# One order of issue exchanged for another in an attention and Mish feed-forward kernel

## The chip, the core and the metric

The kernel runs on one core of one Trainium2 chip. The metric is device time in microseconds (us), from one timed execution to the next of the same program; the kernel before was timed three times, and the median counts. One more execution was recorded by the hardware profiler, and all readings of single instructions come from that one.

A core has engines that run side by side, each through its own list of instructions in the order in which they were issued: PE (TensorE, matrix multiplication; its weight loads are listed as PEld), DVE (VectorE), ACT (ScalarE), POOL (GpSimd) and SP (SyncE, which here only starts transfers). An engine waits at the first instruction of its list whose inputs aren't there; nothing behind it can overtake.

## The reference, cut to what matters

Attention over hashed buckets, then a feed-forward layer with the Mish function between two matrices:

```python
B, H, S, D = 4, 8, 768, 64                       # q, k, v: float32; proj: 64 x 6
q_bits = (q @ proj > 0); k_bits = (k @ proj > 0) # 6 bits: one of 64 buckets
mask = q_bucket[:, :, :, None] == k_bucket[:, :, None, :]
scores = where(mask, q @ k.T / sqrt(D), -1e9)
attn = exp(scores - scores.max(-1)); attn /= attn.sum(-1) + 1e-9
x = (attn @ v) as 3072 x 512
h = x @ w_in                                     # 512 x 2048, float64 in memory
g = h * tanh(log1p(exp(h)))                      # Mish
out = g @ w_out                                  # 2048 x 512, float64 in memory
```

## The kernel before, in words

Every matrix operand is held as two float16 parts, a high part ("hi") and the remainder ("lo"), and a product is made of two or three matmuls of these parts. The two weight matrices arrive as 64-bit numbers, and are put together into float32 on the chip first (operations `w_u`, `w_sign`, `w_low`, `w_join`), then scaled by a power of two and split (`square`, `st`, `half`, `w_hi`, `w_lo`). The same scaling and splitting is done for q, k and v (`k_hi`, `k_lo`, and so on). A bucket's bits go through a small matmul (`hp`), and turn into columns of large constants beside q and k (`bits`), so that the mask is part of the score matmul.

The attention is cut into 96 slots. A slot n has two heads and 128 queries against 768 keys. In the order of the data:

- `S`n, on PE: 8 matmuls into the PSUM tile `ps_s`, of which there is only one (line 802). The next `S` has to wait until both `exp` of this one have read it.
- `max`, on DVE: a maximum over 2 x 768 scores (line 809), and from it a scale and a bias (lines 812 and 815). There are two forms of the last part: for both heads in one instruction each, or for one head at a time, with twice the instructions.
- `exp`, twice, on ACT (line 825), each with its row sums. Results go to a ring of three buffers `pb`.
- `sums` and `rv` (lines 838 to 847): one over the sums.
- `hi`, twice: the scaled float16 part, on ACT (line 368), POOL (line 366) or DVE (line 369), to a ring of three buffers `hl`.
- `lo`, twice: the remainder. For the first ten slots PE makes it (`diag`, `lo_pe`, lines 415 and 416) and ACT or DVE copies it out of PSUM. From slot 10 on it is one instruction on DVE (line 387), or two on POOL (lines 393 and 394).
- `ptturn`, twice: a transposing transfer from `hl` to `PT`, started by SP (line 428).
- `V`p, on PE, for each two slots: 36 matmuls (line 882); `x_hi` on ACT and `x_lo` on DVE take the result out.

Eight slots make a unit of 256 tokens, and there are 12 units. A unit then goes through the feed-forward layer in eight groups m of 256 hidden columns: `H`m on PE (24 matmuls, lines 913 to 915), `mish` on ACT (line 931), `g_hi` on ACT, POOL or DVE, `g_lo` on DVE (line 387), and `O`m0 and `O`m1 on PE (6 matmuls each, lines 951 to 953). `exp` and `mish` are in different function tables of ACT; each change between them costs a table load, which the trace shows as an instruction of its own.

The program doesn't issue anything while it describes this. Each operation is entered into a list with the operations it must follow and with its alternatives, one for each engine or form that can do it. The description makes 2,671 operations, numbered in the order of the description. `ORDER` (line 87) is a text that was written by a planner ahead of time: a row of these numbers, each with a letter for its alternative (none for the first, b, c, d). `Plan.ordered` goes through that text and issues, without any other reordering:

```python
for w in ORDER.split():
    n, a = (int(w[:-1]), "abcd".index(w[-1])) if w[-1].isalpha() else (int(w), 0)
    o = self.ops[n]
    assert all(q in done for q in o.preds), o.name
    done.add(o)
    yield o.alts[a][2]
```

So `ORDER` sets the order of each engine's list, the order of SP's transfers, and the engine of every operation that has a choice. For instance, "24c" is the split of q for the first unit on its third alternative, DVE. `S8` is 344 in that row, `S20` is 758, `S92` is 2515, and the first feed-forward matmul `H0` is 470.

Of the kernel before, what the change touches and what calls it, by code (L numbers as in the profile page):

```python
# [92 lines left out]
121 193c 148c 227b 159 194 77 166b 206b 195b 108 147 149 150 197 182 160 257 198 183 207 196 201 78 161 228 199b
202 162 208 184b 203 209b 210 167 173 164 151 180 174 94 200 229 217b 221 213b 186 211b 176b 238 222 214 212c
204 223 218 185b 163 187 224 175c 219b 241c 253 258b 215 165 242 177 239 240 188 254b 216 189 243b 259 420 178
249b 245 230 260 255 246 256 244c 286 220 250 251 287 237 282 270d 271 272c 274c 231 191 275 283b 299 233c 236
232 247 343 276 285 288c 278 284 269 300 252 234 190 289 248 277 297 302 318b 273b 303 305b 301 235b 298 310c
192 314 290 279 304b 280 315b 306b 261 291 292 281 311 316 307 308 309 293c 262 317 294c 268 312b 319 320b 295
331c 263 264 378 344 296 379 332 333 321 334c 359 339b 330 340 335b 380 322 265 360 341 336 345 329 313 346 348c
361 337 347 381 323 362 266 267 324 338 363 325c 326b 364c 374 327 382 342 349 389 383 366b 370 407b 350c 390  # L100
365c 328 384 351 386c 371 367 408b 352 385b 409 353 372b 368 354 369 355 375 447b 376 432 410 356c 377 387 448
391 449c 392 394c 450 433 411 357 419 466 388 418 403 395b 434 393b 358 467 399 412 413 451 396 485b 414 468
415b 421 404 486 457 400 397 487 422 456 405 406 416 401b 511c 373 417 469 398 443 435b 488 470 402 489 495 436
423 437b 494 444 438 439 478 445 446 425 441 440 458c 481 512 426 513 424 479 459 480 461b 482 471 474 442 460
452 464 475 453 427 462 472c 465 428 535 514 473 631 483 476 490 430 429 484 546b 496b 463 515 507 454 491 521
497 504 539 498 492 499 508 505 500 509 510 455 520 522c 547 502 501 540 431 523 531 541 548b 516 524 549 525
517 550 493 477 557 551 558b 552 553b 526 559 518b 530 554 560b 503 532 542 519 561 593 562 536 556 506 533 543
537b 563 564 624 555 545 534 565c 583c 544 567c 575 566 584 576 579 528 538 585b 568 614 586 569 527 587 571b
580b 570 529 581 582 606c 588 589 592 590c 573 597b 591 594 598 595c 607 572 599b 577 596 628 578 629 600 609b
574 608 601 632 633 610 634 651 620 630 602 635 603 652 617 636 611 616 612 621 653 604c 637 746 654 605 647 613  # L110
638b 675 648 655 615b 656 640 625 657c 676 721 679 649 618 659 650 619 683 622c 623 626c 677b 690 658 641 666
667 639 684 660 668 686 627 685 642b 687 720 691 645 674 644 688 692 670 750 693 643 694c 671 696 697 661 662
689 703c 669 663 747 680 664 704 716 678 646 717b 751 665 711 672b 748 706 705 681b 754 698 709 682 712 707 718
719 695b 699 735d 736 758 713 701 722 723 749 752 724 700 673 759 737 760 725 739 726 743 744 728 770 773c 714
708 710 702 774 761 785 755 753 740 738c 775 789 771 776 729 762 766 772 727b 783 730 778c 763 756b 777 791 741
784 790 757 767 786b 731 732 779 792 733 793 745 764b 787 742 788 734 812 794 795c 820 797 804d 815 765 805 780
816b 823b 821 814 798 781b 813 715 838 806 870 768b 817 808 818 807c 824 769 825b 782 822 809 796 839 840 810b
826 834 835 827c 819 829 836 865 799 866 837 800 841 924 878 802 833 874 879b 867 811 828b 831b 871 857 801 842
843 875 868b 844 832 882 853 858 869 830 803 880 859b 854 861 846 886 847 883 887 881 855 872c 903 884 890 905
860 885 873 891 895d 896 892 862 845b 863b 904 848 906 925 897 907 849 899 918 908 876 898 926 927 909c 856 928c  # L120
850 864 937 930 910 917 888b 901b 911 920 921 900 922 851 889 913 931 938 919 939 902 852 914 923 943d 912 940
915b 951 1144 944 932 954 941b 955 945c 969 956 947 957 916 933 970 929b 946c 973 977 949 950 978b 934 948 971b
966 972 1262 974 1055 981 952 1100 958 959 967 975 960c 877 962 979 893c 980 961 982 1000 983b 992b 1001 963
1101 976 894 964 985 1002 986 993 994c 1014 984 1003 1102 995b 1103 996 965 1004 998 1005 987c 1015 935 1104c
988 1021 1016 989 990 1017 1006b 1007 1008b 1033 1010b 1018b 1046 997 991 999 1020 1106b 1019 1025 1051 1034
1026 1009c 1011 1052 1047 1048 1035b 1028b 1012b 1027c 1029 1036 1037 1031 1022 936 1023 1038 1143 1060 1049c
1024 1039 1105b 1056 1107 1145 1013 1061 1050 1064 1053b 968 1062 1080 1065 1030 1108 1057 1041 1079 1032 1040b
1263 1109 1058 1054 1042 1059 1292 1068 942 1081 1071b 1044 1066b 1264 1072 1093 953 1063 1265 1073 1069 1094
1082b 1110 1075 1083 1095 1111 1043 1074b 1325 1084 1113 1070 1266 1067 1045 1085b 1086 1087 1076 1077 1096 1267
1125 1097 1089 1114 1088c 1098 1099 1078 1115 1091 1112 1090 1117c 1140 1118 1116 1128 1150 1141 1119b 1129 1121  # L130
1126b 1268 1092 1146 1120c 1123 1130 1142 1131 1270b 1132c 1154 1166 1151 1147 1155 1148c 1133 1232 1134c 1167
1152 1149 1136 1122 1135c 1269c 1153 1156 1157 1169d 1170 1162 1124 1138b 1178 1163 1171b 1127 1177 1137 1168
1179 1158 1139 1159 1180b 1172b 1192 1175b 1191 1173 1160c 1164b 1224 1181 1182 1194 1183 1225 1161 1193 1199
1195 1184 1196 1185c 1165 1228 1187 1226c 1197 1202c 1211 1200 1201 1174 1186b 1203 1210 1176 1189 1198 1204
1206b 1212b 1188 1205 1213 1214 1237 1233 1190 1229 1227 1215b 1207 1208 1216 1218b 1256 1217b 1230b 1238 1234b
1245 1231 1219 1209 1235 1236 1246 1241 1221 1239 1248b 1242 1258 1247 1285 1249 1223 1257 1240 1259b 1243c 1244
1220 1250 1251 1286 1252 1271 1222 1260 1287 1254b 1261 1288 1277d 1293 1272 1278 1273 1279 1253 1289 1255 1281
1290 1274 1291 1280b 1305 1306 1282 1307 1317 1320 1309 1310 1312 1283b 1308 1321 1311c 1313 1284 1322 1350 1323
1315 1275 1351 1339d 1340 1354 1341b 1294 1358 1318b 1295 1347 1355 1324 1352 1296b 1362 1314 1348 1359b 1316
1349 1298 1353 1356 1366 1343 1360 1370 1342c 1345 1383 1474 1357 1363 1367 1299 1364 1365 1361 1373c 1385 1371  # L140
1368b 1276 1344 1372 1375c 1376 1412 1297b 1326 1300 1377b 1386 1378 1301 1384 1379 1303 1327 1328 1346 1302
# [952 lines left out]
```

## Time and profile before

| | before |
|---|---|
| device time, median of 3 runs (lowest to highest) | 886.45 us (886.02 to 888.27) |
| span of the profiled execution, first to last instruction | 887.0 us |
| busy time of PE, DVE, ACT, POOL in it | 823.2, 679.0, 606.0, 301.4 us |
| mean granted clock of TensorE | 0.987 of full speed |

The profiled execution's own time is its span, 887.0 us; the median of the timed runs is 0.55 us below it, and nothing of the execution lies outside the span that this argument needs. A row of the groups of instructions reads: line of the kernel, engine, operation, output <- inputs, shapes, count | busy us, mean ns of one | idle time of the engine just before them, and what ended most of it. A row of the stretches gives for a stretch of time its length, then the busy us and the count of instructions of each engine (PE, PEld, DVE, ACT, POOL), the granted TensorE clock, the busy share of the transfer engines, and GB/s. A row of a timeline gives start, duration, engine, line, operation and names.

### The profile page before, as it was taken

To read this page: it belongs to the slowest core of one execution; us is meant where nothing else is said; L and a number is where in the kernel's file an instruction comes from. 1 tells how busy PE (TensorE), PEld (TensorE's weight loads), DVE (VectorE), ACT (ScalarE), POOL (GpSimd) and SP (SyncE) were. 2 spreads that over 40 slices of the span, in tenths; PEclk is the share of its full clock that TensorE was granted. 3 is DMA by queue.
4 is the path that set the end of the run, shared out by engine and by line. 5 is a ranking of instruction groups with operands and counts; after the bars stand their busy time and mean duration, and the time that the engine had idled before them with its cause. 6 is when DMAs were issued, how large, how long until landed. Compare 5 with 4: busy or idle time off the path is not lost.

```text
span 887.0 us, 17219 instructions
## 1 busy us (share of the span) xinstructions
PE 823.2 (93%) x6626; PEld 547.1 (62%) x6626; DVE 679.0 (77%) x1323; ACT 606.0 (68%) x963; POOL 301.4 (34%) x279
## 2 busy tenths in 40 slices
PE   3689988889999999999899999999989999999998
PEld 1355555566666767656657666766756766776665
DVE  3688799998778888778888987678888777776421
ACT  6686878887788676768677667756867657666410
POOL 3353442223442515333144413443332523335000
PEclk9799999999999999999999999999999999999999
DMA  8999989689999797567999968669999667566300
GB/s 266 270 230 246 213 220 207 143 193 175 219 154 180 132 210 141 105 119 149 209 208 185 184 108 155 108 124 219 211 184 166 121 130 138 102 106 134 72 24 24
DMA packets 432690, 143.75 MB, mean 162 GB/s; under 512 B 402912, under 2 KB 423392, under 8 KB 432608
## 3 DMA queue, kind: packets, MB, share of 16 engines
q1 hardware_dynamic: 432608, 142.65, 81.5%
q8 instruction: 52, 0.85, 0.4%
q14 instruction: 30, 0.25, 0.1%
HBM read 35.65 MB, written 6.29 MB: 47 GB/s over the span
## 4 chain that ended last, share of the span: by engine, by line
PE 50%; DVE 14%; DMA 8%; ACT 7%; issue 5%; POOL 2%; SPq 1%; ACTq 0%; DVEq 0%; POOLq 0%
PE ps_s L802 9%; PE ps_acc L913 6%; PE ps_acc L914 6%; PE ps_acc L915 6%; PE ps_t L882 6%; PE ps_o L951 6%; PE ps_o L953 5%; PE ps_o L952 5%; DVE svb L809 5%; ACT pb L825 4%; DMA PT<-hl 3%; DMA QT<-tok 3%; DMA KT<-tok 2%; DVE hl L387 2%; DVE svb L812 1%
## 5 line engine op out<-in xcount | busy, mean ns | idle before, releaser
L825 ACT ACTIVATE pb<-ps_s,svb 128x768 f32<-128x768 f32 x192 | 189.1, 987 | 118.9 <-DVE svb L815 104.0
L913 PE MATMUL ps_acc<-X,wi 128*128 128x256 f16 x768 | 211.2, 275 | 2.5 <-ACT ffb L931 2.4
L914 PE MATMUL ps_acc<-X,wi 128*128 128x256 f16 x768 | 211.2, 275 | 0.0
L915 PE MATMUL ps_acc<-X,wi 128*128 128x256 f16 x768 | 211.2, 275 | 0.0
L809 DVE TENSOR_REDUCE svb<-ps_s 128x2 f32<-128x1536 f32 x96 | 168.5, 1755 | 41.8 <-PE ps_s L802 39.8
L802 PE MATMUL ps_s<-KT,QT 128*128 128x512 f16 (+1 forms) x768 | 142.8, 329 | 17.7 <-ACT pb L825 16.2
L953 PE MATMUL ps_o<-wo,ffb 128*128 128x512 f16 x384 | 145.5, 379 | 0.4 <-DVE ffb L387 0.3
L951 PE MATMUL ps_o<-wo,ffb 128*128 128x512 f16 x384 | 145.8, 380 | 0.0
L952 PE MATMUL ps_o<-wo,ffb 128*128 128x512 f16 x384 | 145.5, 379 | 0.0
L387 DVE SCALAR_TENSOR_TENSOR hl<-pb,svb,hl 128x768 f16<-128x768 f32 x125 | 135.6, 1090 | 6.5 <-POOL hl L366 3.5
L366 POOL TENSOR_SCALAR hl<-pb,svb 128x768 f16<-128x768 f32 x63 | 65.2, 1036 | 221.1 <-DVE svb L847 88.7
L802 PEld LDWEIGHTS <-QT 128*128 128x128 f16 x768 | 73.2, 98 | 73.6 <-issue 27.6
L882 PE MATMUL ps_t<-PT,VT 128*64 128x256 f16 x1728 | 103.7, 274 | 1.3 <-DVE hsum L670 0.7
L931 ACT ACTIVATE ffb<-ps_acc,smalls 128x512 f32<-128x512 f32 x96 | 64.1, 684 | 59.1 <-PE ps_acc L915 52.6
L882 PEld LDWEIGHTS <-VT 128*64 128x64 f16 x1728 | 91.1, 110 | 18.5 <-issue 18.4
L387 DVE SCALAR_TENSOR_TENSOR ffb<-ffb,smalls 128x512 f16<-128x512 f32 x96 | 73.9, 774 | 27.1 <-POOL ffb L366 20.3
L368 ACT ACTIVATE hl<-pb,svb 128x768 f16<-128x768 f32 x73 | 67.5, 929 | 29.0 <-DMA PT<-hl 16.4
L914 PEld LDWEIGHTS <-wi 128*128 128x128 f16 x768 | 75.7, 99 | 17.6 <-issue 3.7
L913 PEld LDWEIGHTS <-wi 128*128 128x128 f16 x768 | 75.7, 99 | 13.1 <-issue 1.6
L915 PEld LDWEIGHTS <-wi 128*128 128x128 f16 x768 | 75.8, 99 | 9.4
L394 POOL TENSOR_TENSOR hl<-pb,hl 128x768 f16<-128x768 f32 x47 | 79.8, 1697 | 3.9
L393 POOL TENSOR_SCALAR pb<-pb,svb 128x768 f32<-128x768 f32 x47 | 46.3, 986 | 90.4 <-ACT hl L368 53.1
(177 smaller groups left out, 1086.9 us busy)
## 6 DMA issues: line engine op xcount, KB each, us to landing
out_dram<-ffb SPq DMA_DIRECT2D x24, 256.0 KB, 3.0
stg<-in_k_dram SPq DMA_DIRECT2D x12, 384.0 KB, 4.4
stg<-in_v_dram SPq DMA_DIRECT2D x12, 384.0 KB, 4.1
stg<-in_q_dram SPq DMA_DIRECT2D x9, 512.0 KB, 5.1
wi<-in_moe_w_in_dram SPq DMA_DIRECT2D x7, 512.0 KB, 4.1
wo<-in_moe_w_in_dram SPq DMA_DIRECT2D x6, 512.0 KB, 5.2
stg<-in_moe_w_out_dram SPq DMA_DIRECT2D x6, 512.0 KB, 5.7
PT<-hl SPq DMA_TRANSPOSE x192, 4.0
```

The costliest lines, as they stand in the source:

```text
L387: return [("DVE", 215 + 1.035 * n, port(lambda: nc.vector.scalar_tensor_tensor(out=dst, in0=src, scalar=sc, in1=hi, op0=ALU.mult, op1=ALU. ...
L394: nc.gpsimd.tensor_tensor(out=dst, in0=src, in1=hi, op=ALU.subtract)
L802: nc.tensor.matmul(ps_s[:, hh * S + c0 * P:hh * S + c1 * P], QTb[:, u % 2, sl, qi], KTb[:, j, sl, hh * NCH + c0:hh * NCH + c1].rearrange(" ...
L809: nc.vector.tensor_reduce(out=sv[:, 0], in_=ps_s.rearrange("p (h e) -> p h e", h=2), axis=AX.X, op=ALU.max, negate=True)
L825: EXP[n, hh] = op("exp", [("ACT", 1075, lambda hh=hh, t=t: nc.scalar.activation(pb[:, t], ps_s[:, hh * S:(hh + 1) * S], AF.Exp, bias=sv[:, ...
L882: nc.tensor.matmul(pv[hh * D:(hh + 1) * D, 0:256], vt[:, w, hh * NCH + c], pt[:, hh, a * NCH + c].rearrange("p s t -> p (s t)"), start=(x ...
L913: nc.tensor.matmul(o, wh, X[:, 0, c], start=(c == 0), stop=False)
L914: nc.tensor.matmul(o, wh, X[:, 1, c], start=False, stop=False)
L915: nc.tensor.matmul(o, wl, X[:, 0, c], start=False, stop=(c == NCC - 1))
L951: nc.tensor.matmul(PS[f"o{s}"], gh, wo[:, g, 0, f2], start=first, stop=False)
L952: nc.tensor.matmul(PS[f"o{s}"], gh, wo[:, g, 1, f2], start=False, stop=False)
L953: nc.tensor.matmul(PS[f"o{s}"], gl, wo[:, g, 0, f2], start=False, stop=last)
```

## The change

The text of `ORDER` is replaced as a whole. The description of the operations, their instructions, what each must follow, the tiles and the rings stay as they are, so the instructions of PE and the transfers are the same set. The diff has some 120 lines on each side that look alike; these are the first of both sides and the last:

```diff
 ORDER = """
-3 12 1 6 0 7 8 2 13 14 9 53 10 79 54 17 18 20 21 19 35 15 4 5 24c 63 22 11 25 16 23 56 26 48b 55 99 47b 38b 111c
-60 36b 64 27 65 37c 28 59 66 89b 91 80c 112 92 39 81b 29 82 40 41 30 156 83 31 32 33 113b 42 67 43 44 49 68 45
...
-2628 2631 2629 2630 2632 2633b 2639 2640 2643 2615 2634 2644 2641 2642 2645c 2646 2659 2660 2647 2651 2648 2649
-2652 2650 2653 2662 2661 2655 2654 2664 2663 2656 2657c 2658 2665 2668 2666b 2669b 2667 2670
+12 7 6 156 4 3 13 8 17 14 53 54 15 55 56 60 16 57 20 21 0 1 2 9 5 10 18 19 24 35 26c 27 22 23 28b 36c 63 64
+38c 65 66 48c 99 79 67 111b 37c 39 40 68 25 80c 81c 11 29 30 47c 49 92 31 33 91 58 41 42 32 43 44 59 112b 113
...
+2646 2656 2657c 2652 2653c 2658 2615 2618 2659 2660 2661 2662 2654 2663 2664 2665 2666b 2667 2668 2669b 2670
 """
```

Counted over the two texts, these are the choices that differ most (number of operations in each place, before -> after):

| operation | ACT | DVE | POOL |
|---|---|---|---|
| `hi` (192) | 73 -> 55 | 56 -> 51 | 63 -> 86 |
| `lo` from slot 10 on (172) | - | 125 -> 91 | 47 -> 81 |
| `g_hi` (96) | 35 -> 19 | 29 -> 43 | 32 -> 34 |
| remainders of k, q, v and weights, `k_lo` `q_lo` `v_lo` `w_lo` (48) | - | 43 -> 27 | 5 -> 21 |
| high parts `k_hi` `q_hi` `v_hi` `w_hi` (60) | 23 -> 13 | 24 -> 19 | 13 -> 28 |
| `w_u`, `w_low` (34) | 16 -> 11 | 9 -> 8 | 9 -> 15 |
| `diag` (32) | 15 -> 7 | 7 -> 13 | 10 -> 12 |
| `max`, both heads at once / one at a time | - | 47 / 49 -> 67 / 29 | - |

In ACT's new list a change between `exp` and `mish` occurs 91 times, in the old one 75 times. The relative order on PE changes too: `H`, `O`, `V` and `S` follow one another in another sequence, with the first `H` after `S11` in both. Of the 350 transfers that SP starts, 67 stand in the same place of its list.

More of the change, by code (lines that the diff above doesn't have):

```diff
@@ L93 @@
[L93 to L117, printed above, removed]
@@ new lines @@
+811 814 819 836 837 840 857c 799 800 801 869 865 878 872 802 831b 924 841 842 843 858 879b 859 880 861 881
+895c 896 745 803 830 860 832 844 846b 886 833 890 905 882 903 891 847 863 897c 899 892 906b 848 845 887 873
+849 862 864 898b 893 901 900 902 925 883 904 926 917 918 907 908 927 884b 909c 853 885 910 920 937 938 919 911
+888b 928 921 922 913 930b 931 914 1100 889 850 912c 923 939 940 943c 944 945c 954 955b 947b 957 915 956 894
+973 854 855 856 958b 877 851 946b 969 949b 974 970 971 977 916 948 715 852 932 978 933 959 960b 962 929c 972
@@ new lines @@
+1402 1520 1504 1569 1521 1513 1522 1523 1447 1448 1543c 1494 1484c 1449 1485 1403 1445 1525 1512b 1515b 1544
+1488c 1489 1518 1554 1519 1537 1526 1573 1555 1319 1514 1516 1545b 1547b 1546 1527 1528c 1451 1450 1452 1548
+1557 1556 1558d 1477 1453 1559 1577 1566 1570 1581 1454 1574 1549 1530 1531 1578 1575 1585 1579 1455 1567b
+1571c 1541c 1560b 1562b 1580 1561 1550 1563 1532 1551 1542 1592 1593 1533 1572 1602 1603 1529 1564b 1456 1552
+1586 1582 1583 1604 1594c 1576 1535 1595c 1596 1587b 1584 1600 1601 1589 1590 1591 1565 1700 1615 1614 1605
@@ new lines @@
+2174 2049 2158b 2051 2119 2137 2126 2177 2114 2116 1949 2146b 2149 2076 2150 2148 2127 2050 2170 2171 2159
+2160 2178 2128b 2130b 2161b 2179 2162 2180 2192b 2193 2166 2185 2054 2181 2055 2056 2172 2343 2202 2052 2163
+2131 2194b 2182 2186 2195 2189 2190 2167 2129c 2151 2203 2191 2344 2196b 2205 2093c 2094 2164 2197 2165 2251
+2201 2132 2198b 2199 2300 2133 2204 2152 2206c 2183b 2207 2175 2176 2134 2141 2187 2135 2209b 2217 2218 2219
+2208b 2210 2220 2225 2226 2184 2212b 2200 2215 2222 2223 2227 2301 2234 2224 2142 2136 2211 2255 2188 2235b
@@ new lines @@
+2366 2334 2351 2320 2336 2357 2367 2358 2362 2295 2348c 2368 2352 2323b 2349 2356 2369 2370 2153 2168 2337
+2372 2375b 2379 2363 2359 2341b 2353 2325 2378 2324 2380 2339 2381 2424 2371b 2360 2373 2382 2383 2384 2326
+2392 2376 2374 2394 2361 2395 2385b 2386 2396 2399 2377 2428 2387b 2388 2397 2389b 2402b 2310 2403 2411 2390
+2312 2412b 2391 2400 2429 2425 2441 2437 2413 2430c 2401 2426c 2427 2404b 2406b 2405b 2364c 2408 2414 2415c
+2433 2365 2416 2417c 2407 2327 2418 2434 2419b 2435 2436 2445 2393 2446 2421b 2342 2409 2420 2422 2398 2410
```

180 lines of the change are left out of this document (94 added, 86 removed).

## The prediction

> **What bounds the kernel now.** I read the page first, for the engines' shares of the profiled execution.
>
> ```profile
> span 887.0 us, 17219 instructions
> PE 823.2 (93%) x6626; PEld 547.1 (62%) x6626; DVE 679.0 (77%) x1323; ACT 606.0 (68%) x963; POOL 301.4 (34%) x279
> ```
>
> PE is busy for 823.2 of 887.0 us. The change leaves PE's instructions as they are, so the most that an order can give is what PE idles, 63.8 us, and part of that is the wait for the first loads. So the second view is where PE idles. I cut the span at three score operations: `S8`, `S20` and `S92` (8 matmuls of line 802 each, counted from the start).
>
> ```profile
> 89.12 1.46 PE L802 MATMUL ps_s<-KT,QT 128*128 128x512 f16 x8
> 209.09 1.46 PE L802 MATMUL ps_s<-KT,QT 128*128 128x512 f16 x8 [0.84 <-ACT pb L825]
> ```
>
> ```profile
> 0.00:89.10 89.10, 63.06 (x368) 34.99 (x369) 61.29 (x146) 63.25 (x110) 36.00 (x40) 0.92 1.06 253
> 89.10:209.10 120.00, 103.69 (x776) 66.66 (x775) 108.67 (x205) 101.54 (x157) 40.10 (x29) 0.96 0.88 192
> 209.10:790.60 581.50, 564.20 (x4781) 383.56 (x4781) 469.96 (x905) 405.11 (x647) 207.49 (x194) 1.00 0.85 158
> 790.60:887.00 96.40, 92.21 (x706) 61.85 (x703) 39.12 (x67) 36.07 (x52) 17.85 (x18) 1.00 0.31 67
> ```
>
> PE idles 26.0 us in the first stretch, 16.3 in the second, 17.3 in the third (3%), 4.2 in the last. In the second stretch DVE is the fullest engine: 108.7 of 120 us (91%), ahead of PE (86%) and ACT (85%), while POOL is at 33%. That stretch is bounded by DVE with ACT close behind; the third is bounded by PE. The third view is what ends PE's waits in the steady part.
>
> ```profile
> L825 ACT ACTIVATE pb<-ps_s,svb 128x768 f32<-128x768 f32 x192 | 189.1, 987 | 118.9 <-DVE svb L815 104.0
> L809 DVE TENSOR_REDUCE svb<-ps_s 128x2 f32<-128x1536 f32 x96 | 168.5, 1755 | 41.8 <-PE ps_s L802 39.8
> L802 PE MATMUL ps_s<-KT,QT 128*128 128x512 f16 (+1 forms) x768 | 142.8, 329 | 17.7 <-ACT pb L825 16.2
> L882 PE MATMUL ps_t<-PT,VT 128*64 128x256 f16 x1728 | 103.7, 274 | 1.3 <-DVE hsum L670 0.7
> ```
>
> `S` waits 16.2 us in all for `exp` to have read the one score tile; `exp` in turn waits 104.0 us for the scale, line 815. `V` hardly waits at all (1.3 us), so the whole way from `exp` over `hi`, `lo` and the transposing transfers is early enough today.
>
> **The change, part by part.** *Work that changes its engine.* Prices are these rows:
>
> ```profile
> L387 DVE SCALAR_TENSOR_TENSOR hl<-pb,svb,hl 128x768 f16<-128x768 f32 x125 | 135.6, 1090 | 6.5 <-POOL hl L366 3.5 <-ACT hl L368 2.3
> L394 POOL TENSOR_TENSOR hl<-pb,hl 128x768 f16<-128x768 f32 x47 | 79.8, 1697 | 3.9
> L393 POOL TENSOR_SCALAR pb<-pb,svb 128x768 f32<-128x768 f32 x47 | 46.3, 986 | 90.4 <-ACT hl L368 53.1 <-DVE svb L841 11.0 <-DVE hl L369 10.1
> L366 POOL TENSOR_SCALAR hl<-pb,svb 128x768 f16<-128x768 f32 x63 | 65.2, 1036 | 221.1 <-DVE svb L847 88.7 <-DMA PT<-hl 57.1 <-DVE hl L387 18.8
> L368 ACT ACTIVATE hl<-pb,svb 128x768 f16<-128x768 f32 x73 | 67.5, 929 | 29.0 <-DMA PT<-hl 16.4 <-DVE svb L847 8.0 <-ACT pb L825 1.6
> L369 DVE TENSOR_SCALAR hl<-pb,svb 128x768 f16<-128x768 f32 x56 | 36.3, 649 | 5.2 <-DMA PT<-hl 4.5
> L368 ACT ACTIVATE ffb<-ffb,smalls 128x512 f16<-128x512 f32 x35 | 25.0, 715 | 0.3
> L369 DVE TENSOR_SCALAR ffb<-ffb,smalls 128x512 f16<-128x512 f32 x29 | 16.1, 557 | 17.3 <-ACT ffb L931 17.0
> L387 DVE SCALAR_TENSOR_TENSOR tok<-stg,smalls,tok 128x768 f16<-128x768 f32 x11 | 11.2, 1015 | 0.3
> ```
>
> Over the program: DVE loses 34 `lo` (34 x 1.09 = 37 us) and 16 remainders of k, q, v and weights (at 1.015, or a third more for the wider ones: some 18), five `hi` (3) and five other casts (3), and gains 14 `g_hi` (8): about -53. POOL gains 34 `lo` of 0.986 + 1.697 = 2.68 us (91), 23 `hi` (24), 16 remainders (at 2.68 or a third more: 48) and 15 high parts and some weight steps (20): 301 becomes about 485 us. ACT loses 18 `hi` (17), 16 `g_hi` (11) and some 20 prep operations at about 0.93 (19).
>
> *`max`.* Twenty pairs go from four small instructions to two:
>
> ```profile
> L815 DVE TENSOR_TENSOR svb<-svb 128x1 f32<-128x1 f32 x98 | 25.3, 286 | 0.0
> L812 DVE TENSOR_SCALAR svb<-svb,smalls 128x1 f32<-128x1 f32 x98 | 16.4, 209 | 1.8
> L812 DVE TENSOR_SCALAR svb<-svb,smalls 128x2 f32<-128x2 f32 x47 | 15.9, 339 | 1.7
> L815 DVE TENSOR_TENSOR svb<-svb 128x2 f32<-128x2 f32 x47 | 11.8, 251 | 1.6
> ```
>
> That is 0.99 us against 0.59, so -8 us on DVE (679 to about 618), on the way from `S` to `exp`.
>
> *Table loads.* 75 become 91.
>
> ```profile
> 249.31 0.19 ACT L825 ACTIVATION_READ_ACCUMULATOR pb<-ps_s,svb 128x1 f32 x1
> 249.51 1.28 ACT L931 ACT_TABLE_LOAD   x1
> 250.81 1.33 ACT L931 ACTIVATE ffb<-ps_acc,smalls 128x512 f32<-128x512 f32 x2
> ```
>
> A load costs 1.28 us and touches both neighbours, so 16 more cost ACT 20.5, and its net is 606 - 47 + 20.5, about 580 us. The Trainium skill (ScalarE: Activation LUTs, What ACT_TABLE_LOAD costs) adds a drain of about 1.38 us to each load, 2.66 together; by that ACT would gain nearly nothing (-4), but the rows here leave no gap for it, so I keep 1.28.
>
> *The second stretch* (between tokens 344 and 758 of each text). DVE loses 7 `lo` (7.6), 4 wide remainders (at 1.35: 5.4), 4 `w_hi` and 2 `w_u` (4.2) and small things (3.3) and gains 2 `hi` and 3 `w_low` (3.5): 108.7 - 17 = 91.7. ACT loses 7 `hi` (6.5) and 6 `diag`, 2 `w_low` and casts (10): 85. POOL gains 6 `lo` (16.1), 4 wide remainders (at 3.58: 14.3), 4 `hi` (4.1) and weight steps: 78. PE has 3.4 us less there (one `V` and one `O` come later; they are only moved) and would be the fullest, at 100.3. If it then idled 3%, as in the third stretch, 13 of its 16.3 idle us go.
>
> *Against it: POOL and DVE get in each other's way.*
>
> ```profile
> 335.91 1.52 DVE L815 TENSOR_TENSOR svb<-svb 128x2 f32<-128x2 f32 x1
> 335.77 1.64 POOL L394 TENSOR_TENSOR tok<-stg,tok 128x768 f16<-128x768 f32 x1
> 418.39 2.14 DVE L387 SCALAR_TENSOR_TENSOR hl<-pb,svb,hl 128x768 f16<-128x768 f32 x1
> 418.07 1.64 POOL L394 TENSOR_TENSOR hl<-pb,hl 128x768 f16<-128x768 f32 x1
> L815 DVE TENSOR_TENSOR svb<-svb x145: 146/160/1569, 32.3 to 821.3; 128x1 f32<-128x1 f32 x98, 128x2 f32<-128x2 f32 x47
> ```
>
> Line 815 works for 0.16 us (its median) but took 1.52 when a POOL instruction had begun before it, ending with it (337.43 against 337.41). Line 387 ended 0.82 us after POOL's release, where the whole takes 1.0: it runs after POOL, save 0.2 us. So DVE's two-input and scaling instructions and POOL take turns. In the second stretch:
>
> ```profile
> 89.10:209.10 120.00, 33.49 (x33) 0.96 0.88 192
> 89.10:209.10 120.00, 12.99 (x18) 0.96 0.88 192
> 89.10:209.10 120.00, 14.49 (x12) 0.96 0.88 192
> ```
>
> (lines 387, 369 and 561 of DVE alone) these are 61 us; less 18 of what leaves, and with POOL's 78, the two need 121 us of turns. With 0.2 us of overlap for each of some 100 instructions it is 102, which fits into 112 us at 91%, not into 107. So I take -8 for the stretch, between -13 (no collisions) and +1 (121 us in full).
>
> By the Trainium skill (SBUF — State Buffer, Who interferes with whom) the pair of ports is held for the whole instruction and the other engine fully blocks. By that the sum of turns, 121 us, would stand; the trace agrees that they take turns, but shows the 0.2 us.
>
> *The first stretch.* The thirteen loads ahead of the first transposing transfer are the same number in both. ACT's list up to `S8` gets some 8 us shorter and POOL's 22 longer. I take -2 (by the ACT work ahead of the first `exp`), between -5 and +3 (q's first split moves from DVE to POOL, 1.04 for 0.65 at the width of the rows, and two loads now stand between the first transposes).
>
> *The third stretch.* After `S`, `max` (1.76), scale (0.59 to 0.99) and two `exp` (about 2.1) take 4.6 to 5 us, in which PE needs other work. From `S12` on I added up what PE has between each two `S`.
>
> ```profile
> 790.45 0.27 PE L915 MATMUL ps_acc<-X,wi 128*128 128x256 f16 x1
> 790.56 1.46 PE L802 MATMUL ps_s<-KT,QT 128*128 128x512 f16 x8
> 480.48 2.09 PE ps_t L882 x36
> ```
>
> A matmul of 256 columns takes its place for 0.11 us (the second row is `S92`), so an `H` of 24 is 2.6 us, an `O` of 6 with twice the columns 1.3, and a `V` is 2.1 by the chain of waits. Before, 48 of 83 gaps hold under 6 us and 13 hold 9 or more; after, 32 and 1. Measured against 5.5 us the missing work falls from 19 to 11 us: of 16.2 us of waiting, 6 may go. But lines 815 and 812 wait for POOL longer: 98 x 0.126 + 47 x 0.09 + 47 x 0.11 = 22 us at POOL's 301, so 35 at 485. Of these 13, a quarter is on the path (23 of 96 `S` waited), so +3. Heads with `hi` and `lo` both on POOL go from 18 to 48 and take 7.4 us for a slot; with the scale, `exp` and
>
> ```profile
> PT<-hl SPq DMA_TRANSPOSE x192, 4.0
> ```
>
> a transfer of 4.0 us and its issue, `V` needs 18 us after its last `S`, and PE's list has 16.6 to 34.9 (median 24.7; before 15.4 to 36.0, 26.1): late at most in a few places by 1.7. Together I take -3, between -9 (half of 17.3) and +11 (all 13 on the path, -2). The last stretch has 4.2 us of idle and the same work after `S92`: 0.
>
> **Sum.** -2 - 8 - 3 = -13 on the profiled 887.0: 874. The median of the runs is 0.55 below that execution; I leave it at 874. Its own range is 866 to 881.
>
> **Rivals.** (a) *All the relief arrives*: -5 - 13 - 9 gives 860. For it: DVE at 91% is the plain bound of the second stretch, and the gaps are more even. Against: POOL at 78 of 107 us collides. (b) *No change*, 886: what ends waits is not the engines but transfers. For it: the transfer engines are 0.88 busy in the second stretch and 1.06 in the first. Against: with 51 instead of 48 transfers in the stretch it could still shrink to 120 x 0.88 x 51/48 / 1.06 = 106. (c) *Slower: turns between POOL and DVE set the pace.* Its place is the scale, lines 812 and 815, ahead of every `exp`. If the turns stay whole, the second stretch takes 121 (+1), and the 13 us of longer waits before `exp` come through in full: with -2 at the start 887 + 1 + 13 - 2 = 899. It decides once `S` waits for `exp` for more than today's 16.2 us, from where each further us is paid; the mean of line 815 would be above 0.35 us then, from 0.27. For it: `exp` waits 104.0 us for line 815 already. Against: most such waits are hidden behind other PE work. That the text is replaced and nothing happens can't be: each list is issued from it.
>
> **How the numbers follow.** Forecast 0.48, (a) 0.16, (b) 0.12, (c) 0.22, else 0.02. The range 858 to 895 goes from just below (a) to just under (c); the sum of all good ends is 860, of all bad ones 902. A measurement tells about 0.3% (2.7 us) from no change. Faster is the forecast and (a) with what is left: 0.66; same is most of (b): 0.11; slower 0.23.
>
> **What would show it.** Right: `S8` to `S20` in about 112 us with DVE near 92 busy; POOL near 485 us over the span, 91 table loads, `S` waiting about 13 us for `exp` in all. Wrong: that stretch at 120 or more with POOL fuller than DVE; line 815 above 0.35 us in the mean with `S` waiting over 16 us; `V` waiting for transposing transfers; PE idle in the third stretch above 17 us.

## The result and the profile after

The new order is slower: 929.31 us in the median of four runs (926.11 to 929.99), against 887.29 (886.02 to 888.27) for the old one, a ratio of 1.046 with a 95% interval of 1.044 to 1.0485. That is 42 us more, where 12 fewer were forecast. The profiled execution was the fastest of the four (926.11 us), with a span of 924.3, so the views below account for 37.3 of the 42 us. Nothing but `ORDER` differs; its new text is two lines longer, so that line 815 of before is 817 here, 812 is 814, 387 is 389, 825 is 827, 802 is 804.

The first view is the engines' shares on the page of the kernel after.

```profile
span 924.3 us, 17257 instructions
PE 832.3 (90%) x6626; PEld 550.2 (60%) x6626; DVE 719.5 (78%) x1246; ACT 578.8 (63%) x920; POOL 498.8 (54%) x422
```

POOL and ACT came out as forecast (498.8 for about 485, 578.8 for about 580). DVE didn't: it has 77 instructions fewer and 40 us more busy time, 719.5 instead of some 618. PE's 6626 matmuls take 9.1 us more at a lower granted clock, and PE idles 92.0 us instead of 63.8. These two are the 37.3 us by which the profiled spans differ.

The second view cuts the span of the kernel after at the same score operations, `S0`, `S8`, `S20` and `S92`. (Columns: the stretch, its length, then PE, PEld, DVE, ACT and POOL busy, the clock, the transfers' share, GB/s.)

```profile
0.00:25.20 25.20, 12.52 (x59) 6.17 (x60) 8.72 (x34) 12.75 (x24) 11.63 (x14) 0.81 0.96 270
25.20:101.40 76.20, 58.01 (x350) 32.21 (x351) 67.33 (x124) 42.22 (x72) 49.15 (x42) 0.84 0.95 206
101.40:226.10 124.70, 99.99 (x733) 64.47 (x732) 114.15 (x188) 88.97 (x142) 78.81 (x64) 0.96 0.83 187
226.10:827.90 601.80, 569.16 (x4811) 386.08 (x4811) 492.89 (x844) 400.46 (x634) 337.68 (x285) 0.99 0.80 153
827.90:924.30 96.40, 92.63 (x682) 61.27 (x680) 36.42 (x61) 34.36 (x50) 21.56 (x19) 1.00 0.29 62
```

Against before, the part up to `S8` is 12.3 us longer (101.4 for 89.1), the second stretch 4.7 (124.7 for 120.0), the third 20.3 (601.8 for 581.5), the last nothing. In the second stretch PE and POOL are where the prediction put them (99.99 for 100.3, 78.81 for 78), and DVE, which was to fall from 108.67 to 91.7, rose to 114.15. Of the 12.3 us ahead of `S8`, 7.5 are more PE work (70.53 us for 63.06; 409 matmuls for 368, so some of it only stands earlier) and 4.8 more idle time.

The third view is the same groups of instructions that the prediction priced.

```profile
L827 ACT ACTIVATE pb<-ps_s,svb 128x768 f32<-128x768 f32 x192 | 189.1, 988 | 125.9 <-DVE svb L817 91.2 <-DVE hl L389 15.6 <-DVE smalls L459 7.6
L396 POOL TENSOR_TENSOR hl<-pb,hl 128x768 f16<-128x768 f32 x81 | 137.2, 1694 | 6.8
L814 DVE TENSOR_SCALAR svb<-svb,smalls 128x2 f32<-128x2 f32 x67 | 39.9, 596 | 2.4
L817 DVE TENSOR_TENSOR svb<-svb 128x2 f32<-128x2 f32 x67 | 30.7, 458 | 2.3
L817 DVE TENSOR_TENSOR svb<-svb 128x1 f32<-128x1 f32 x58 | 14.3, 275 | 0.0
L814 DVE TENSOR_SCALAR svb<-svb,smalls 128x1 f32<-128x1 f32 x58 | 9.7, 209 | 1.0
L827 ACT ACT_TABLE_LOAD x45 | 57.7, 1283 | 52.0 <-DVE svb L817 42.7
L933 ACT ACT_TABLE_LOAD x46 | 59.0, 1283 | 7.7 <-DVE ffb L389 4.8 <-DVE smalls L443 2.2
```

The two-column form of the scale, of which the new order has 67 in place of 47, went from 339 to 596 ns on line 814 and from 251 to 458 on line 817. On line 814 it took 228 to 230 ns in the 14 cases that overlap no instruction of POOL, and 693 ns in the mean in the other 53. The four rows of the scale add up to 94.6 us, against 69.4 before. Twenty pairs fewer were to take 8 off and the longer waits to add 13, which is 74. There are 91 table loads, as forecast, at 1.28 us. Table load and `exp` together now wait 133.9 us for line 817 (91.2 + 42.7).

The fourth view is one such wait, in the timeline of the kernel after, once on DVE and once on POOL.

```profile
147.00 1.51 DVE L814 TENSOR_SCALAR svb<-svb,smalls 128x2 f32<-128x2 f32 x1
148.55 0.83 DVE L817 TENSOR_TENSOR svb<-svb 128x2 f32<-128x2 f32 x1
```

```profile
146.37 2.12 POOL L396 TENSOR_TENSOR wo<-stg,wo 128x1024 f16<-128x1024 f32 x1
148.47 0.91 POOL L395 TENSOR_SCALAR pb<-pb,svb 128x768 f32<-128x768 f32 x1
```

Line 814 waits for the end of one POOL instruction (148.51 against 148.49), line 817 for the end of the next (both at 149.38). The two instructions that hold back `exp`, 0.39 us of work, took 2.4 us.

The last view is PE's waits in the third stretch, first of before and then of after (columns: total us, times, longest).

```profile
PE ps_s L802 <- ACT pb L825: 9.2, 18, 1.3
```

```profile
PE ps_s L804 <- ACT pb L827: 23.6, 26, 4.7
```

PE idles 15.3 us more in that stretch (32.6 for 17.3), and 14.4 of these are `S` waiting for `exp`; the other 5.0 of its 20.3 us are PE's work, with 30 more matmuls. `V` waits for a transposing transfer once, for 0.6 us.

### The profile page after: what moved, and what is told of

It is laid out like the page before. It is cut to its first block, busy times and chain, and to the rows that moved or that the text cites. A ratio compares the mean times of both kernels' runs of the same rounds, so it can differ in the third digit from the quotient of the medians.

```text
span 924.3 us, 17257 instructions
## 1 busy us (share of the span) xinstructions
PE 832.3 (90%) x6626; PEld 550.2 (60%) x6626; DVE 719.5 (78%) x1246; ACT 578.8 (63%) x920; POOL 498.8 (54%) x422
## 5 line engine op out<-in xcount | busy, mean ns | idle before, releaser
L827 ACT ACTIVATE pb<-ps_s,svb 128x768 f32<-128x768 f32 x192 | 189.1, 988 | 125.9 <-DVE svb L817 91.2
L804 PE MATMUL ps_s<-KT,QT 128*128 128x512 f16 (+1 forms) x768 | 146.7, 335 | 33.9 <-ACT pb L827 28.5
L368 POOL TENSOR_SCALAR hl<-pb,svb 128x768 f16<-128x768 f32 x86 | 89.9, 1048 | 138.3 <-DVE svb L849 71.6
L396 POOL TENSOR_TENSOR hl<-pb,hl 128x768 f16<-128x768 f32 x81 | 137.2, 1694 | 6.8
L395 POOL TENSOR_SCALAR pb<-pb,svb 128x768 f32<-128x768 f32 x81 | 84.8, 1046 | 84.4 <-ACT hl L370 39.8
L804 PEld LDWEIGHTS <-QT 128*128 128x128 f16 x768 | 75.5, 99 | 91.6 <-issue 45.1
L389 DVE SCALAR_TENSOR_TENSOR hl<-pb,svb,hl 128x768 f16<-128x768 f32 x91 | 107.7, 1186 | 7.3 <-POOL hl L368 3.7
L884 PE MATMUL ps_t<-PT,VT 128*64 128x256 f16 x1728 | 106.1, 277 | 7.2 <-DVE ho L459 5.7
L389 DVE SCALAR_TENSOR_TENSOR ffb<-ffb,smalls 128x512 f16<-128x512 f32 x96 | 84.4, 884 | 18.2 <-POOL ffb L368 11.4
L827 ACT ACT_TABLE_LOAD x45 | 57.7, 1283 | 52.0 <-DVE svb L817 42.7
L916 PEld LDWEIGHTS <-wi 128*128 128x128 f16 x768 | 75.2, 98 | 17.3 <-issue 2.6
```

The lines of the kernel that those rows point to most:

```text
L389: return [("DVE", 215 + 1.035 * n, port(lambda: nc.vector.scalar_tensor_tensor(out=dst, in0=src, scalar=sc, in1=hi, op0=ALU.mult, op1=ALU. ...
L396: nc.gpsimd.tensor_tensor(out=dst, in0=src, in1=hi, op=ALU.subtract)
L804: nc.tensor.matmul(ps_s[:, hh * S + c0 * P:hh * S + c1 * P], QTb[:, u % 2, sl, qi], KTb[:, j, sl, hh * NCH + c0:hh * NCH + c1].rearrange(" ...
L827: EXP[n, hh] = op("exp", [("ACT", 1075, lambda hh=hh, t=t: nc.scalar.activation(pb[:, t], ps_s[:, hh * S:(hh + 1) * S], AF.Exp, bias=sv[:, ...
L884: nc.tensor.matmul(pv[hh * D:(hh + 1) * D, 0:256], vt[:, w, hh * NCH + c], pt[:, hh, a * NCH + c].rearrange("p s t -> p (s t)"), start=(x ...
L916: nc.tensor.matmul(o, wh, X[:, 1, c], start=False, stop=False)
```

## The experiments

Four theories stood at the start. *Turns*: DVE's instructions wait out POOL's long ones, above all at the scale, and `exp` with them. *Sequence*: the new row of operations is worse whatever the engines. *Lateness*: POOL does its work too slowly, and what needs its results waits. *Loads*: the 91 table loads stand on the path. Each run was compared with runs of the kernel before on the same chip (886.8, 886.8, 887.4, 886.7 and 885.7 us in the five groups); "over before" below is the difference of the two medians.

### Sequence and engines taken apart

`new_seq_old_eng` has the new row of numbers with the old letters, `old_seq_new_eng` the reverse:

```diff
-... 20 21 0 1 2 9 5 10 18 19 24 35 26c 27 22 23 28b 36c
+... 20 21 0 1 2 9 5 10 18 19 24c 35 26 27 22 23 28 36b
```

> The new sequence of operations with the engines and forms of the old one. POOL is back at about 300 us. Theory 1 and theory 3: most of the 42 us goes, 887 to 900. Theory 2: 920 or more.

> The old sequence with the new engines and forms. POOL at about 490 us. Theory 1: about as slow as the changed kernel or slower, 915 to 950, lines 812 and 815 waiting 50 us or more for POOL. Theory 2: 885 to 900. Theory 3: 915 to 950 too, but with V or the transposing transfers as what PE waits for.

Measured: 1056.21 (169 us over before; ratio 1.1915, 1.1886 to 1.1944) and 1005.83 (119 over; 1.1338, 1.1305 to 1.1371). Neither half can be had by itself: `S` waits 87.9 and 52.7 us for `exp`, for 28.5 in the kernel after. A likely reason, not followed further, is that an engine that can't overtake, with work on it that the row wasn't made for, holds up everything behind. So the loss can't be shared out between sequence and engines in this way, and the theory of the sequence is neither borne out nor refuted.

### The scale freed of POOL

Both forms of the scale become one instruction for each head with a column as the scalar operand, and the product goes by such a scalar instead of two tensors (`new_free`; the same in the old order is `old_free`):

```diff
-for w in (slice(0, 1), slice(1, 2)) if single else (slice(0, 2),):
+for w in (slice(0, 1), slice(1, 2)):
     nc.vector.tensor_scalar(out=sv[:, 1, w], in0=sv[:, 0, w], scalar1=HALF, scalar2=sg[:, j:j + 1],
                             op0=ALU.is_le, op1=ALU.mult)
-for w in (slice(0, 1), slice(1, 2)) if single else (slice(0, 2),):
-    nc.vector.tensor_tensor(out=sv[:, 2, w], in0=sv[:, 0, w], in1=sv[:, 1, w], op=ALU.mult)
+for w in (slice(0, 1), slice(1, 2)):
+    nc.vector.tensor_scalar(out=sv[:, 2, w], in0=sv[:, 1, w], scalar1=sv[:, 0, w], scalar2=None, op0=ALU.mult)
```

> The changed kernel, with the scale behind each maximum made of four one-column instructions, the product by a scalar pointer instead of a second tensor. The trace of the changed kernel shows that one-column instructions with a scalar pointer never wait for POOL, and that lines 814 and 817 wait 52 us for it in all. Theory 1 (turns between POOL and DVE on the way from S to exp): 929 falls by 20 us or more, to 900 to 910, and the wait of S for exp from 28.5 us to under 15. Theory 2 (the sequence itself is worse, whatever the engines): 924 to 930. Theory 3 (POOL is late with hi and lo): 922 to 930, since these stay on POOL.

> The kernel before with the same four one-column instructions. Theory 1: the 24 us that lines 812 and 815 wait for POOL there go; a quarter is on the path, so 878 to 884. Theories 2 and 3: 886 to 890, a little slower at most for the twenty more small instructions.

Measured: 911.99 (25.2 over before; 1.0292, 1.0277 to 1.0308) and 883.89 (2.9 under before; 0.9965, 0.9949 to 0.998). The first lies a little above the 900 to 910 of the theory of turns, and `S` still waits 19.7 us for `exp` there (28.5 in the kernel after), not under 15. The scale's two lines, first in the kernel after and then in `new_free` (count: shortest, median and longest in ns):

```profile
L814 DVE TENSOR_SCALAR svb<-svb,smalls x125: 202/228/1641, 34.0 to 856.0; 128x2 f32<-128x2 f32 x67, 128x1 f32<-128x1 f32 x58
L817 DVE TENSOR_TENSOR svb<-svb x125: 145/160/1609, 34.9 to 856.2; 128x2 f32<-128x2 f32 x67, 128x1 f32<-128x1 f32 x58
```

```profile
L814 DVE TENSOR_SCALAR svb<-svb,smalls x192: 202/210/216, 35.3 to 843.6; 128x1 f32<-128x1 f32 x192
L817 DVE TENSOR_SCALAR svb<-svb x192: 202/208/215, 35.6 to 843.8; 128x1 f32<-128x1 f32 x192
```

Not one of 384 instructions was held up, beside the same POOL work (502 us), and the longest of them took 216 ns instead of 1641. So 17 of the 42 us are the scale's turns, nearly all of them behind `S8` (`S8` is 11.7 us late here, 12.3 in the kernel after).

The waiting didn't all go. An estimate: take each DVE form's own short duration (the tenth percentile of its instructions) as its work, and what is above it as waiting. Then the kernel after waits 52 us at the scale and 94 at DVE's other instructions, and `new_free` 2 and 113. Some of the freed time was lost again at other instructions.

The Trainium skill has the rule behind this (SBUF — State Buffer, Who interferes with whom): a DVE instruction shares ports with POOL only if it has two SBUF inputs or runs in a mode that takes both port pairs; its page VectorE: DVE Perf Modes (What auto-detection actually checks) ties that mode to a single source and to the size of the outermost dimension that isn't one. The rows agree where two columns wait on line 814 and where both forms wait on line 817, with two inputs. That one column doesn't wait on line 814 is read from the rows alone.

### POOL given more work in the old order

`old_plus_copy` adds six small copies on POOL behind each slot's second `exp` from slot 12 on, `old_plus_fill` ten small fills; their results aren't used:

```diff
 for fn in plan.ordered():
     fn()
+    if fn in at:
+        for _ in range(6):
+            nc.gpsimd.tensor_scalar(out=extra, in0=extra, scalar1=1.0, scalar2=1.0, op0=ALU.mult, op1=ALU.mult)
```

> The kernel before, with six more POOL instructions behind the second exp of each slot from 12 on (a 128 x 128 tile copied onto itself, about 0.37 us each; nobody waits for them): some 185 us more of POOL, as the change has, without moving any operation. Theory 1 (turns): lines 812 and 815 wait 40 us or more for POOL instead of 24, the kernel gets 8 to 20 us slower, 895 to 907. Theory 3 (POOL late for its own work): the same time as with the fills of the run beside it, whatever that is.

> The kernel before with ten POOL fills of a 128 x 256 float16 tile in the same places (about 0.21 us each by the fill in the trace): about the same time on POOL, but nothing is read. Theory 1: instructions of DVE with two tensors (lines 815, 387) do not wait for a fill, so less than half of the loss of the copies, 887 to 895. Theory 3: the same loss as with the copies.

Measured: 890.8 (4.0 over before; 1.0046, 1.0028 to 1.0063) and 905.47 (18.7 over; 1.0212, 1.0174 to 1.0251). The added groups, of the first and of the second kernel:

```profile
L1070 POOL TENSOR_SCALAR extra<-extra 128x128 f32<-128x128 f32 x504 | 228.5, 453 | 35.5
```

```profile
L1070 POOL MEMSET extra<- 128x256 f16 x840 | 281.1, 335 | 43.7
```

With 228.5 us of short copies POOL is as full as in the new order (526.9 us), for a tenth of the loss and less than the 895 to 907 that the theory of turns gave. By the estimate above DVE's waiting rises only from 59 us before to 69 with the copies and 71 with the fills (147 in the kernel after). So the price of the turns doesn't follow POOL's busy time, by which the prediction scaled it; it depends on how long a single instruction holds DVE up, and where it stands.

The fills cost more than the copies, against what was expected of them. Turns are hardly the reason: DVE's waiting is nearly the same with both, and line 817, with two tensors, took at most 162 ns in all 29 cases that began under a fill. The fills take more of POOL's time (3.4 us a slot for 2.7), and `S` waits 25.0 us for `exp`, for 18.0 with the copies. That POOL's own work comes too late behind them, which is the theory of lateness, would fit, but isn't shown.

### First stretch and rest

`old_head_new_tail` is the old row up to `S8` and then what is left of the new one in its order; `new_head_old_tail` is the reverse.

```diff
+k = position of S8 in the first row
+row = first[:k] + [t for t in second if number(t) not in first[:k]]
```

> The old text up to S8, then all that is left in the new order with the new choices. If the 12 us that the changed kernel loses before S8 are a loss of their own (conversions on POOL and DVE at the same time): 912 to 920. If the late start only shows early what any new order pays anyway: 925 to 932. If the seam itself costs, above 932.

> The complement: the new text up to S8, then the rest of the old one. If the loss before S8 stands by itself: 887 + 12, so 896 to 903. If the new head has work done ahead that the old tail then saves: 885 to 895.

Measured: 918.04 (31.3 over before; 1.035, 1.0317 to 1.0382) and 899.05 (12.3 over; 1.013, 1.0099 to 1.0161). The two add up to 43.6 of 42.0, so the parts lose nearly independently of each other. (The old row up to `S8` doesn't bring `S8` all the way back: it comes at 93.8 us in `old_head_new_tail`, for 89.1 before.)

### Table loads ahead of their wait

The load for `exp` stands behind the wait of its `exp`; `new_preload` issues it right behind the last `mish`. `new_two` has this and the freed scale, `old_two` the same two in the old order.

```diff
     fn()
+    if fn in early:   # the last mish before an exp
+        nc.scalar.preload_act_table_set("exp_and_others")
```

> The changed kernel, with each table load for exp issued right behind the last mish instead of in front of the exp, so that it does not stand behind the wait for the scale. In the changed kernel 45 such loads, 27 of them with the engine idle for the scale just before (42.7 us; before the change 7 and 6.6 us). Theory 4 (a load of 1.28 us between the scale and exp is on the way from S to exp): a third to a half of 27 x 1.28 reaches the end, 911 to 919. If that way does not matter: 926 to 931.

> The changed kernel with the one-column scale and the early table loads together. Theories 1 and 4 add up where S waits for exp: 897 to 906; if they shorten the same wait, 906 to 912.

> The kernel before with the one-column scale and the early table loads. Only 11 loads waited there, so 2 to 4 us below the 884 of the one-column scale alone: 879 to 883; 884 to 887 if the loads were hidden.

Measured: 925.08 (37.7 over before; 1.0425, 1.0407 to 1.0443), 912.28 (24.9 over; 1.0278, 1.0259 to 1.0297) and 884.36 (3.0 under; 0.9966, 0.9953 to 0.9978). The loads' idle time of 52 us is gone, and the time fell by 4 us; beside the freed scale it fell by nothing. The loads waited, but little waited for them. That theory falls.

### POOL's long instructions cut

`new_split` cuts each remainder on POOL: the scaling in two pieces, the subtraction in three or four.

```diff
-nc.gpsimd.tensor_scalar(out=src, in0=src, scalar1=sc, scalar2=1.0, op0=ALU.mult, op1=ALU.mult)
-nc.gpsimd.tensor_tensor(out=dst, in0=src, in1=hi, op=ALU.subtract)
+for y in range(2):
+    nc.gpsimd.tensor_scalar(out=cut(src, y, 2), in0=cut(src, y, 2), scalar1=sc, scalar2=1.0,
+                            op0=ALU.mult, op1=ALU.mult)
+k = 3 if n == 768 else 4
+for y in range(k):
+    nc.gpsimd.tensor_tensor(out=cut(dst, y, k), in0=cut(src, y, k), in1=cut(hi, y, k), op=ALU.subtract)
```

> The changed kernel, with POOL's remainders in pieces: the scaling in two, the subtraction in three (four for the wider ones). POOL gets about 60 us more to do, but holds no turn for longer than about 0.6 us instead of 1.5. Theory 1 (DVE waits out long POOL instructions): DVE's waits fall, 905 to 925. Theory 3 (POOL is late with its results): 935 or more.

Measured: 921.63 (34.3 over before; 1.0382, 1.0362 to 1.0402). The page and two groups of this kernel:

```profile
PE 835.0 (91%) x6626; PEld 551.0 (60%) x6626; DVE 692.0 (75%) x1246; ACT 580.1 (63%) x920; POOL 574.8 (63%) x736
```

```profile
L402 POOL TENSOR_TENSOR hl<-pb,hl 128x256 f16<-128x256 f32 x243 | 170.9, 730 | 0.0
L820 DVE TENSOR_SCALAR svb<-svb,smalls 128x2 f32<-128x2 f32 x67 | 26.2, 390 | 2.4
```

POOL does 76 us more (a remainder's subtraction is 2.19 us in three pieces for 1.69 in one), and the kernel is 8 us faster: DVE's busy time falls by 27.5 us, and its waiting, by the estimate above, from 147 to 118, since it waits out pieces of 0.7 us. That is against lateness as the main cause, and for turns.

### Both cures together, and in the old order

`new_free_split` has the freed scale and the cut instructions, `old_head_new_free_split` the old row up to `S8` as well, `old_free_split` both edits in the old order. The edits are those shown.

> Both edits in the new text: the scale freed of POOL, and POOL's remainders cut into pieces. By the traces the freed scale took 12 us out of the part after S8 and next to nothing before it, the pieces took 4 us before S8 and 1 after. If the two heal different waits they add: S8 at +8 us against the kernel before, the end at +20, 907. If what is left of the loss is the same turn-taking on DVE's longer instructions, which pieces of 0.4 us leave short, it goes further: 900 or below. If both heal the same waits: 912, as with the freed scale alone.

> The old text up to S8, the new one behind it, with both edits: what is left of the second and third stretch's loss. By adding: 12 to 13 us over the kernel before, 900. If the loss behind S8 is all turn-taking: within 5 us of the kernel before, 892. If it is the new sequence: 905 or more.

> The same two edits in the old text, which had 884 with the freed scale alone. POOL gets about 25 us more work by the pieces. If long holds cost there too: 880 to 883. If the old text has no such waits left: 884 to 886.

Measured: 909.27 (22.6 over before; 1.0265, 1.0238 to 1.0292), 904.26 (17.6 over; 1.0209, 1.0182 to 1.0236) and 886.91 (0.3 over; 1.0006, 0.9994 to 1.0018). The two edits overlap: 17 and 8 give 19 together. The old first stretch gives 5 more, less than its 12: cutting had already brought `S8` to 96.2, and it still comes at 92.0 for 89.1. The second stretch is back at 120.6 us there (92.0 to 212.6), for 120.0 before. In the old order cutting costs the 3 us that the freed scale gives. The stretch from `S20` to `S92` in `old_head_new_free_split`, and PE's and ACT's waits there:

```profile
212.60:806.00 593.40, 567.88 (x4811) 385.71 (x4811) 463.32 (x944) 402.45 (x634) 395.23 (x526) 0.99 0.83 155
```

```profile
PE ps_s L805 <- ACT pb L829: 17.7, 19, 3.3
...
ACT pb L829 <- DVE svb L818: 51.4, 24, 6.1
ACT L829 <- DVE svb L818: 30.7, 20, 4.0
ACT pb L829 <- POOL hl L397: 19.4, 10, 5.2
```

This stretch is 11.9 us longer than before, 3.7 of it PE's (30 more matmuls stand in it) and 8.2 idle; `S` waits 8.5 us more for `exp`. With the turns at the scale gone, `exp` waits in ten places for POOL's remainder (line 397) to be done with one of the three `pb` buffers, which in the kernel after shows with 0.9 us. A run with a fourth `pb` buffer would have told what that is worth; it wasn't tried. Turns away from the scale are a rival: by the estimate above DVE waits 79 us at its other instructions in this run, for 36 before.

### Four remainders of the first stretch put back

`new_four_back` gives two `k_lo`, one `v_lo` and one `q_lo` ahead of `S8` back to DVE.

```diff
-... 100 101b 102b 109 ... 158b 159b 184 186b 90b
+... 100 101b 102 109 ... 158b 159 184 186 90
```

> The new text with four remainders of the first stretch (two of k, one of v, one of q) back on DVE, as they were before: POOL has some 11 us less to do there, DVE some 4.5 us more. If POOL's long instructions between S0 and S2 make the first stretch late: S8 at +6 us or less instead of +12, the end at 921 to 924. If it is the sequence, or DVE's own list there: S8 at +12 or later, 929 or more.

Measured: 929.68 (43.0 over before; 1.0495, 1.0446 to 1.0544), no gain, with `S8` at 103.4. `S2` came 5.6 us sooner (45.5 for 51.1), and then `S3` stood 7.1 us for a transposing transfer of k, and came later than in the kernel after (60.6 for 58.4). PE's longest wait between them in this kernel:

```profile
PE ps_s L799 <- DMA KT<-wo: 7.1, 1, 7.1
```

The first 50 us of before and of after show what differs there.

```profile
0.00:50.00 50.00, 27.26 (x144) 14.39 (x145) 28.53 (x73) 34.52 (x60) 17.08 (x21) 0.86 1.02 268
```

```profile
0.00:50.00 50.00, 23.34 (x100) 11.14 (x101) 31.11 (x65) 20.65 (x39) 33.64 (x30) 0.66 0.90 241
```

Conversions that ACT did (34.52 to 20.65 us) are on POOL (17.08 to 33.64), and 100 matmuls are done by then instead of 144. In the kernel after, between `S0` and `S2`, the timeline shows what stands behind them (start, duration; in brackets the idle time before and what ended it):

```profile
36.58 1.99 POOL L396 TENSOR_TENSOR wo<-PT,wo 128x768 f16<-128x768 f32 x1
...
37.13 2.52 DVE L563 SCALAR_TENSOR_TENSOR wi<-wo,wi 128x1024 int32<-128x1024 int32 x1
...
39.57 1.48 DVE L371 TENSOR_SCALAR VT<-wi,smalls 128x768 f16<-128x768 f32 x1
...
41.18 0.87 DVE L843 TENSOR_SCALAR svb<-svb 128x2 f32<-128x2 f32 x1
...
42.17 2.12 DVE L676 TENSOR_SCALAR wo<-hsum 128x72 f16<-128x72 f32 x1
...
45.64 1.22 PE L417 MATMUL ps_l<-pb,ffb 128*128 128x512 f32 x1 [5.10 <-DVE ffb L371]
```

The sums of the first two `exp` (line 843) were ready to be taken at 37.8 and are taken at 41.18, since line 563 (1.21 us in the mean of before) and line 371 run ahead of them and wait for POOL; line 676, 0.19 us in its median, takes 2.12; PE idles 5.10 us. The cut instructions gave 4 us in this stretch, the four remainders nothing; the rest of the 12 us wasn't traced to one place.

### The moved remainders by themselves

`new_free_lo_back` gives every attention remainder its old engine in the new row (47 on POOL instead of 81), `old_free_lo_pool` the new engine in the old row; both have the freed scale. The edit is a letter, "b" or none, at the `lo` operations.

> The new sequence with the freed scale, and with the engine of every attention remainder as it was before (47 instead of 81 of them on POOL); all other engines as in the new text. Beside the freed new text at 912. If the moved remainders themselves are what is left of the loss (POOL's holds, and exp waiting for a buffer that POOL still reads): 900 or below. If the sequence was made for them, and DVE's 37 us more in it are late for exp: 915 to 940.

> The old sequence with the freed scale, and with the engine of every attention remainder as in the new text (81 on POOL), nothing else changed. Beside the freed old text at 884. If the moved remainders by themselves cost what is left: 900 or more. If they only cost in a sequence that makes them late: within 5 us of 884. If they help: below 884.

Measured: 948.64 (63.0 over before; 1.0708, 1.0676 to 1.0739) beside 912 without the edit, and 908.72 (23.1 over; 1.0264, 1.0242 to 1.0287) beside 884. Both are losses, of 37 and 25 us. The move by itself, in the row that was not made for it, costs 25 us though DVE has 34 us less of these instructions (136.0 in `old_free` to 102.4); and in the row that was made for it, taking it back costs more. The groups of `lo` in `old_free_lo_pool`:

```profile
L391 POOL TENSOR_TENSOR hl<-pb,hl 128x768 f16<-128x768 f32 x81 | 140.1, 1729 | 6.8
L384 DVE SCALAR_TENSOR_TENSOR hl<-pb,svb,hl 128x768 f16<-128x768 f32 x91 | 102.4, 1132 | 12.2 <-POOL hl L363 7.9 <-ACT hl L365 2.4 <-issue 1.3
```

The 34 remainders take 2.72 us each on POOL (1.729 for line 391 and 0.995 for line 390) where DVE took 1.09, and those left on DVE get longer (1132 ns for 1093). Against `old_free`, `S` waits 29.8 us for `exp` instead of 13.0, `exp` waits 10.1 us for POOL's remainder instead of 4.5, and DVE's waiting is 76 us by the estimate above instead of 47: lateness and turns grow together. The Trainium skill warns of the exchange in general (Perfetto Trace Analysis, Optimizing Scalar/DVE Operations): DVE and POOL share a read port, so moving work between the two might not help. `old_free_lo_pool` agrees with it; that the reverse move costs too is not explained by it.

## Why the prediction was wrong

The forecast was 874 us, between 858 and 895, with a chance of 0.66 for faster; 929.31 lies 34 us above the range. Step by step:

- *What bounds the kernel.* PE's idle time was read rightly as what an order can win or lose, and DVE as the fullest engine of the second stretch. The reading left out that part of DVE's busy time is waiting for POOL, and that this part grows with what POOL is given to do, so a DVE at 91% isn't relieved by the full amount that leaves it. By the estimate used above, DVE's waits inside its busy time rose from 59 to 147 us, and the rest of it fell from 620 to 573.
- *Second stretch, -8, taken between -13 and +1; measured +4.7.* This is the first wrong step: "With 0.2 us of overlap for each of some 100 instructions it is 102, which fits into 112 us at 91%". PE and POOL came as priced (99.99, 78.81), and ACT within 4 us (88.97). Of the 17 us of relief some 13 did leave DVE's work (100 to 88 us by the estimate), and the turns gave them back: the waits in its busy time went from 8 to 26 us, and it was 114.15 busy instead of 91.7. The sum of turns in full, 121, was worked out, set aside for its lower end, and came nearer. In `new_free_split`, from 96.2 to 217.2, the stretch takes 121.0 even so; there 12.1 of its 22.0 us of PE's idle time end with DVE's results, against 6.1 of 16.3 before. So the 112 failed for more than the scale.
- *Third stretch, -3, between -9 and +11; measured +20.3.* The gain from more even gaps, 6 us, isn't seen, and no run tests it by itself. The price of the turns was mis-sized twice. Their growth was scaled by POOL's total (22 to 35 us): the scale rows measure 94.6 us where 74 followed. And "a quarter is on the path": in the runs, freeing the scale gave 17 us. The extra waits of the scale in the kernel after are about 94.6 - 61.4 = 33 us (61.4 being the old rows less the 8 us); the same edit gave 3 us in the old order, so some 14 of the 33, two fifths, came through. The growth is more than POOL's share; the new order also has 67 of the two-column scales for 47. And POOL's slower heads were priced against `V` alone, not against `exp`, which needs their `pb` buffers back: with both edits and the old head `exp` waits 19.4 us for that.
- *`max`, -8 us on DVE.* This is the step with the wrong sign. Two instructions for four save 0.4 us by the mean rows of before, but both of the two take turns with POOL, while of the four the two on line 812 don't. In the new order the saved time was lost again: 596 + 458 ns are 1.05 us for a two-column pair, 0.97 for the four single ones (2 x 209 + 2 x 275). The row that said so was quoted: line 812 at 209 ns in the one-column form, 339 in the other.
- *First stretch, -2, between -5 and +3; measured +12.3.* `S0` did come 2.3 us sooner (25.2 for 27.5). Then POOL's and DVE's conversions held up `S1` and `S2` (37.8 and 51.1 us, for 34.6 and 41.9). The prediction looked at ACT's list ahead of the first `exp` and at two transfers, and not at what POOL's 22 us would be waited for.
- *Last stretch 0, table loads 91, ACT 580, POOL 485, `V` not late:* right, POOL within 14 us.
- *The rivals.* (c) named the mechanism, the place and the sign by which it would be known: line 815's mean above 0.35 us (45.0 us over 125, 0.36, at line 817) and `S` waiting more than 16.2 us (28.5). Its price, 899, was 30 us short, and its chance, 0.22, too low. (a) and (b) fell: the time rose by 42 us, and transfers are less busy than before (0.83 and 0.80).

What the runs account for of the 42 us: the freed scale 17, the cut instructions 3 more beside it (8 alone), the old first stretch 5 more. 17.6 us are left in `old_head_new_free_split`. There it is `S` waiting for `exp`, later in the new row, partly because POOL still reads `pb`; that POOL's slower remainders make this by themselves is argued from the waits and from `old_free_lo_pool`, and isn't shown, since the reverse edit made the new order worse, and since the turns at DVE's other instructions weren't taken away. It stays open.

## What to carry to other kernels

Before work is moved from DVE to POOL, compare the durations of each DVE form with its own short ones: nearly all of what lies above is waiting for POOL here (142 of the 147 us in the kernel after fall on instructions that overlap one of POOL's). In these runs it grew with the length of POOL's single instructions, and little with POOL's share. Keep the small instructions on the critical path in a form that doesn't take turns; here one column with a scalar operand did it, and the old order with that edit is the fastest version of the study (883.89 us, 0.35% under before, 0.2 to 0.5%; with the early table loads as well, 884.36). An order and a choice of engines that were made together can't be judged in halves: each half alone lost 119 to 169 us here.

## What the runs showed of the hardware

- A one-column DVE instruction with a column as its scalar operand was never held up by POOL (384 of 384 between 202 and 216 ns); the two-column form took up to 1641 ns.
- Short copies on POOL cost little (4 us for 228.5 us in copies of 0.45 us), and cutting instructions of 1.7 us into pieces won 8 us at 76 us more POOL time.
- Fills on POOL, which read nothing, held up no two-tensor instruction of line 817 (at most 162 ns in 29 cases), and still cost more than copies (18.7 us for 4.0). They took 335 ns in the mean for 128x256 f16.
- The granted clock was lower at the start: 0.66 over the first 50 us for 0.86 before, with 100 matmuls for 144. What sets it isn't shown: up to `S0` it was 1.00 in `new_free` and 0.81 in the kernel after, with 57 and 59 matmuls. PE's whole work took 9.1 us more with the same instructions.
